# A recurrent-memory attention block with gMLP: the two halves' value sums side by side, their memory sums in other banks, 20 paired heads of Wo

## The chip, the core and the metric

The kernel runs on one core of a Trainium2 chip. The metric is device time in microseconds (us) of one launch; lower is better. Engines are named as in the profile: PE (TensorE, matmul), PEld (its weight loads), DVE (VectorE), ACT (ScalarE), POOL (GpSimd), SP (which issues DMAs).

## The reference

Two layers, each an attention block A and a gated MLP block B, each behind a layernorm and with a residual. Block A walks through 2048 rows in 64 segments of 32 rows, one after the other, since each takes 8 memory rows from the one before:

```python
for s in range(n_seg):                       # 64 segments, seg_len = 32
    xs = x[:, s * seg_len:(s + 1) * seg_len, :]
    h = jnp.concatenate([mem, xs], axis=1)   # 8 + 32 rows of 512
    q, k, v = h @ Wq, h @ Wk, h @ Wv         # 32 heads of 128
    scores = einsum(q, k) * scale            # masked: memory or not later
    o = softmax(scores) @ v
    o = einsum('bhte,hed->btd', o, Wo)
    mem = o[:, :M, :]                        # 8 rows, for the next segment
    outs.append(o[:, M:, :])
```

Block B is `z = gelu(x @ w_in)`, a spatial product of its normalised second half with `w_sp`, a gate and `w_out`.

## The kernel before

The work of PE, DVE and ACT stands in program order, written out by hand (`manual_schedule`); POOL and SP are ordered by the framework, which also puts in the waits. A PSUM tile of a pool with one buffer takes the banks of the tile before it under the same tag, and its first writer waits until the last reader of that one is done.

A segment (`segment`, called 64 times in each A block) does in order on PE:

1. psQ, psm and psK, later psV: q, k and v of the two halves r of 16 heads each, six products of 16 matmuls (L697), each 128 rows by 32 columns of the array, four side by side. ACT copies each to SBUF (L906), DVE transposes it into QQ or KA (L909).
2. psS, the scores of half 0 (L932, L936), psV (L697, the values of half 1), the scores of half 1. ACT takes Exp of each half (L941), DVE multiplies it with the mask into E (L944). psV goes through a DVE cast to VA.
3. A filler, then for half 0: `sums_memory` (L958, a matmul with ones that sums the softmax's denominators of the memory rows), `pv` (L975, L978, E times V into psO[0]), `memory_out` (ACT Ln and Exp of the sums, L992 and L993, and DVE's multiplication into uT, L994). These matmuls use 64 rows by 128 columns of the array.
4. A second filler, then the same for half 1 and `sums_tokens` (L967, the other denominators, into psT).
5. `wo_pairs` (L777, px): 18 heads of Wo, two heads of two halves side by side, 256 columns; `wo_rest` (L784): the other 14 heads, 128 columns each, into a free corner of psO[0].
6. A third filler. Beside it ACT copies half of px (cross, L1053), takes Ln of psT (Rt, L1055) and Exp of that (L1058); DVE folds px (L873, L875), adds psO's corner (`build_hA`, L880) and transposes the sum into hT (L881). These are the memory rows, and psQ of the next segment needs them.
7. DVE multiplies the token rows (`tok_out` L997, `last_out` L1000) out of psO with Rt.

PSUM: tag att (two banks) holds psQ, psS and psT in turn; attO0 holds psK and psO[0], attO1 psO[1]; accB holds psm, psV, px; accA the fillers' psb.

The fillers are pieces of a generator that `fill` advances. In the first three segments of each 128 rows it is `b_units`, which prepares q, k and v of rows that the next four segments use (six products j, two in a segment); in the fourth it is `y_part` (a piece of Wo's product for the finished rows, tile pwB) or, in four segments of each A block, nothing. `b_units` yields after 4, after 8 more and after 20 more matmuls of a pair of products; the copy out of PSUM (L751 or L758) is put on the list `copies`, which `run(copies)` empties in front of `wo_pairs` and after the third filler.

`spare1`, `spare2` and `spare3` put statistics, sums and layernorms of other rows between these steps, on DVE and POOL.

Of the kernel before, what the change touches and what calls it, by code (L numbers as in the profile page):

```python
# [8 lines left out]
F32 = mybir.dt.float32  # L9
ACT = mybir.ActivationFunctionType  # L10
ALU = mybir.AluOpType
# [3 lines left out]
P = 128  # L15
# [10 lines left out]
LN_EXP_SET = 6  # L26
GELU_SET = 11
WO_LOW = (4, 4, 4, 3)
WO_PAIR = 18
OLD_SIZES = (H * P, 8 * DH, H * 32, H * 32)  # L30
ORDERED = {mybir.EngineType.PE, mybir.EngineType.DVE, mybir.EngineType.Activation}

# [620 lines left out]
def a_block(tc, c, rows, front, MV_in, RS_in, MV_out, RS_out, ahead, wo, S, first):  # L653
    nc = tc.nc
# [5 lines left out]
    with ExitStack() as ctx:  # L660
# [75 lines left out]
        def b_units(tb, early=0):  # L736
            bs = blk_state[tb]
            order = (0, 2, 1, 3, 4, 5) if early else (4, 5, 0, 2, 1, 3)

            for k, j in enumerate(order):  # L740
                now = k < early
                ps = (accB if k % 2 and not (now and j == 5) else accA).tile([P, 512], F32, name="psb")[:]
                for kts in (((0,), (1, 2), (3,)), ((0, 1, 2, 3),))[k % 2]:
                    mm_chunk(ps, lambda kt, cg: bs["hB"][:, kt, :],
                             lambda kt, cg: qk_rhs(w, j, kt, cg) if j < 4 and now else cols_rhs(w, j, kt, cg), kts)
                    if kts[-1] != KT - 1:
                        yield

                def out(k=k, j=j, ps=ps, now=now):
                    if j >= 4:  # L750
                        nc.scalar.copy(bs["VB"][:, :, j - 4, :], ps.rearrange("p (i e) -> p i e", i=4))  # L751
                        if now:
                            ahead.regroup(bs["VB"], bs["VX"], (j - 4,))
                        elif j == 4:
                            store_v(bs)
                        return
                    r = rowsB[:, k % 2, :]
                    nc.scalar.copy(r, ps)  # L758
                    t = bs[("QTB", "KTB")[j // 2]][:, j % 2]
                    if now:  # L760
                        turns.append(lambda: nc.vector.transpose(out=t.rearrange("p a b -> p (a b)"), in_=r))
                    else:
                        nc.sync.dma_start_transpose(out=t.rearrange("p (i g) k -> p i (g k)", g=4), in_=r.rearrange("t (i e) -> t i e", i=4))

                if now or k % 2 == 0:
                    copies.append(out)
                else:
                    copies.insert(0, out)
                if now or k % 2:
                    yield  # L770

        def wo_pairs(px, lhs):

# [26 lines left out]
        def y_part(G, q, last=False):  # L800

            groups = [oBs[G][:, :, 32 * g:32 * g + 32] for g in range(4)]
            if last:
                parts = [[(groups[g], 8 * q + k) for g in range(3)] + [(groups[q], 24 + k)] for k in range(8)]
            else:
                parts = [[(groups[g], 8 * q + k) for g in range(4)] for k in range(8)]
            pwB = accA.tile([P, DM], F32, name="pwB")
            for k, _ in enumerate(wo_last(parts, pwB)):
                if k in (0, 2):
                    yield  # L810

            def add(lo, n, src):
                nc.vector.tensor_tensor(out=yB[G][lo:lo + n, :], in0=pwB[src:src + n, :], in1=yB[G][lo:lo + n, :], op=ALU.add)

            def out():
                n = 96 if last else P
                if q == 0:
                    yB[G] = wk.tile([P, DM], F32, name="yB", bufs=1)
                    nc.vector.tensor_copy(yB[G][0:n, :], pwB[0:n, :])
                else:  # L820
                    add(0, n, 0)
                if last:
                    if q == 2:
                        store_last(G, 0, 64, nc.sync)
                    add(32 * q, 32, 96)
                    if q == 2:
                        store_last(G, 64, 96, nc.sync)
                elif q == 3 and G < NB // 4 - 2:
                    stores.append(lambda: store_last(G, 0, P, nc.sync))
                elif q == 3:  # L830
                    store_last(G, 0, P, nc.sync)

            adds.append(out)
            yield
# [42 lines left out]
        def build_hA(s, pw, t1):  # L877

            t, at = memT[s % 2], 32 * (s % 4)
            nc.vector.tensor_tensor(out=t[:], in0=pw, in1=t1[:], op=ALU.add)  # L880
            nc.vector.transpose(out=rows.hT[s // 4][:, :, at:at + 32], in_=t[:])  # L881

        def store_o(s, pw, t1):

# [4 lines left out]
        def segment(s, fill, spare1, spare2, spare3, tail, loads):  # L889
# [56 lines left out]
            def e_all(e, lo, hi):  # L946

                return e[:, :, 0:160].rearrange("p n (i q) -> p n i q", q=40)[:, :, :, lo:hi]

            def e_own(e, b):  # L950
                return e[:, :, 160:224].rearrange("p n (i b e) -> p n i b e", i=4, b=2)[:, :, :, b, :]

            def sums_memory(r):

                for k in range(2):
                    for g in range(2):
                        e = E[64 * g:64 * g + 64, r]
                        nc.tensor.matmul(psO[r][:, g, 320:384], lhsT=ones[64 * g:64 * g + 64, :], rhs=e_own(e, 0) if k else e_all(e, 0, 8),  # L958
                                         start=(k == 0), stop=True, skip_group_check=True)

            def sums_tokens(ps):

                for k in range(2):
                    for g in range(2):
                        e = E[64 * g:64 * g + 64].rearrange("p r s n -> p (r s) n")
                        o = ps[:, g, :].rearrange("p (n i q) -> p n i q", n=4, i=4)
                        nc.tensor.matmul(o[:, :, :, 24:32] if k else o, lhsT=ones[64 * g:64 * g + 64, :],  # L967
                                         rhs=e_own(e, 1) if k else e_all(e, 8, 40), start=(k == 0), stop=True, skip_group_check=True)

            def pv(r):  # L970

                for i in range(4):
                    for g in range(2):
                        o = psO[r][:, g, 0:320].rearrange("p (s i q) -> p s i q", s=2, i=4)[:, :, i, :]
                        nc.tensor.matmul(o, lhsT=VA[64 * g:64 * g + 64, r, i, :], rhs=E[64 * g:64 * g + 64, r, :, 40 * i:40 * i + 40],  # L975
                                         start=False, stop=True, skip_group_check=True)
                for g in range(2):
                    nc.tensor.matmul(ends(heads40(psO[r][:, g, 0:320])), lhsT=VX[64 * g:64 * g + 64, j4, r, :],  # L978
                                     rhs=E[64 * g:64 * g + 64, r, :, 160:224], start=False, stop=True, skip_group_check=True)
# [7 lines left out]
            def rview(r, lo, hi):  # L987
                return Rt[:].rearrange("p g (r n q) -> p r g n q", r=2, q=32)[:, r, :, :, lo:hi]

            def memory_out(r):  # L990
                rm = Rm[:, r]
                nc.scalar.activation(out=rm, in_=psO[r][:, :, 320:384], func=ACT.Ln)  # L992
                nc.scalar.activation(out=rm, in_=rm, func=ACT.Exp, scale=-1.0)  # L993
                nc.vector.tensor_tensor(out=hview(uT_cur[:], r, 24, 32), in0=oview(r, 0, 8), in1=rm.rearrange("p g (n q) -> p g n q", q=8), op=ALU.mult)  # L994

# [35 lines left out]

            psO = [attO[r].tile([P, 2, 512], F32, name="psO") for r in range(2)]
            Rm = segp.tile([P, 2, 2, 64], F32, name="Rm", bufs=1)
            if not (first and s == 0):
                fill()
            sums_memory(0)
            pv(0)
            memory_out(0)
            spare1(E)
            if not (first and s == 0):  # L1040
                fill()
            sums_memory(1)
            pv(1)
            psT = att.tile([P, 2, 512], F32, name="psT")
            sums_tokens(psT)
            memory_out(1)
            run(copies)
            px = accB.tile([P, 512], F32, name="px")
            wo_pairs(px, uT_cur)
# [31 lines left out]
        if first:  # L1081
            for tb in range(2):
                ln_turn(tb, nc.scalar.copy)
            units, units1 = b_units(0, 6), b_units(1, 2)
            for gen in (units, units1, units):
                for _ in range(4):
                    next(gen)
                    run(turns)
                    run(copies)
                run(turns)  # L1090
        else:
            blk_state[0] = dict(KTB=KTBr[0], QTB=QTBr[0], VB=VBr[0], VX=wo.VX[0])
# [7 lines left out]
            rows.y_load(y, first, nc.gpsimd, rows.pool.tile([P, DM], F32, name="y_x")[:], o)()  # L1100

        def values(units):
            for n in (3, 1):
                for _ in range(n):
                    next(units)
                run(copies)
                yield
# [151 lines left out]
```

## Time and profile before

| | us |
|---|---|
| runs | 1649.05, 1649.40, 1654.26; median 1649.4 |
| profiled execution | 1649.51, span 1647.8 from first to last instruction |
| PE busy | 1590.4 (97%) |
| DVE, ACT busy | 1183.4 (72%), 1072.7 (65%) |
| granted TensorE clock | 0.997 of full speed |
| one regular segment, first psQ to first psQ | 10.16 (310.00 to 320.16) |
| PE, DVE, ACT busy in it | 10.16, 7.18, 8.18 |
| first block B, pz to the next psQ | from 706.80 to 848.50 |

128 segments of about 10.2 us make up most of the time, so 0.04 us in each is about 5 us in all. In the timeline a row gives start, duration, engine, line, what is written and read, the part of the array (128\*32 is 128 rows by 32 columns), the shape and how many such instructions follow each other; behind it, in brackets, the engine's idle time and what ended it. A duration of several matmuls reaches from the first start to the last modelled end, so rows overlap, and it is the starts that tell PE's pace.

### The profile page before, as it was taken

How to read it: one execution, taken by the hardware profiler on the slowest of the kernel's cores; microseconds unless marked ns; L12 is line 12 of the kernel's file. 1: busy time of each engine (PE TensorE's matmuls, PEld its weight loads, DVE VectorE, ACT ScalarE, POOL GpSimd, SP SyncE). 2: the span in 40 equal slices, each digit the busy share in tenths (PEclk: the TensorE clock that was granted, in tenths of full speed). 3: DMA queues.
4: the chain of work that ended last, by engine and by line, in shares of the span. 5: the costliest groups of instructions: out<-in, count | busy, mean ns of one | idle time of the engine just before them, and what ended most of it. 6: DMA issues, size and time to landing. Idle time of an engine off the chain costs nothing.

```text
span 1647.8 us, 87178 instructions
## 1 busy us (share of the span) xinstructions
PE 1590.4 (97%) x39122; PEld 953.7 (58%) x39122; DVE 1183.4 (72%) x2924; ACT 1072.7 (65%) x2278; POOL 289.2 (18%) x604
## 2 busy tenths in 40 slices
PE   4799999999999999999999999999999999999999
PEld 1455555555665666566655565556556666554565
DVE  3677777778887787884467777777788778877722
ACT  2577777777777777661047777777777777776400
POOL 5111111111211122320011111111122112214000
PEclk9999999999999999999999999999999999999999
DMA  9312221212222234276952121112233123335796
GB/s 353 101 42 42 43 42 44 44 42 74 78 55 45 73 84 87 87 190 139 211 168 46 46 45 46 49 46 44 60 88 85 46 58 94 97 63 153 150 198 162
DMA packets 264734, 149.06 MB, mean 90 GB/s; under 512 B 198680, under 2 KB 240784, under 8 KB 264360
## 3 DMA queue, kind: packets, MB, share of 16 engines
q1 hardware_dynamic: 251128, 99.66, 27.6%
q0 software_dynamic: 13232, 43.82, 8.2%
q8 instruction: 307, 5.03, 1.3%
q14 instruction: 67, 0.55, 0.1%
HBM read 59.68 MB, written 37.19 MB: 59 GB/s over the span
## 4 chain that ended last, share of the span: by engine, by line
PE 55%; DVE 2%; issue 0%; ACT 0%; DVEq 0%
PE pg L388 9%; PE psQ L697 7%; PE psK L697 7%; PE psb L697 5%; PE pz L287 5%; PE px L777 4%; PE psm L697 3%; PE psV L697 3%; PE psO L784 3%; PE py L431 2%; PE pwB L796 2%; PE psO L958 1%; PE psO L975 1%; PE psT L967 1%; PE psS L932 1%; PE pw L1211 0%
## 5 line engine op out<-in xcount | busy, mean ns | idle before, releaser
L697 PEld LDWEIGHTS <-hT 128*32 128x32 bf16 x12288 | 339.8, 97 | 299.9 <-DVE hT L881 27.8
L909 DVE STREAM_TRANSPOSE QQ<-rows 128x512 bf16<-128x512 bf16 x256 | 177.6, 694 | 60.0 <-ACT rows L906 59.0
L909 DVE STREAM_TRANSPOSE KA<-rows 128x512 bf16<-128x512 bf16 x256 | 176.0, 688 | 11.6 <-ACT rows L906 6.1
L997 DVE TENSOR_TENSOR uT<-psO,Rt 128x384 bf16<-128x384 f32 x256 | 141.0, 551 | 36.6 <-ACT Rt L1058 35.6
L906 ACT CAST rows<-psQ 128x512 bf16<-128x512 f32 x256 | 142.8, 595 | 28.3 <-PE psQ L697 25.2
L388 PE MATMUL pg<-z,wspT 128*128 128x344 bf16 x1024 | 154.3, 309 | 0.0
L1058 ACT ACTIVATE Rt<-Rt 128x512 f32<-128x512 f32 x256 | 147.2, 622 | 4.0
L697 PE MATMUL psQ<-Wq_sb,hT 128*32 128x512 bf16 x2048 | 136.0, 383 | 10.7 <-DVE hT L881 6.7
L941 ACT ACTIVATE S<-psS 128x224 bf16<-128x224 f32 x256 | 91.5, 358 | 80.6 <-PE psS L936 80.5
L994 DVE TENSOR_TENSOR uT<-psO,Rm 128x128 bf16<-128x128 f32 x256 | 74.7, 292 | 96.6 <-ACT Rm L993 95.9
L867 POOL COPY KX<-old 128x128 bf16<-128x128 bf16 x128 | 70.2, 548 | 392.3 <-PE psS L936 272.7
L777 PEld LDWEIGHTS <-uT 128*32 128x32 bf16 x4608 | 110.5, 96 | 47.5 <-DVE uT L994 31.7
L697 PE MATMUL psQ<-Wk_sb,hT 128*32 128x512 bf16 x2048 | 135.7, 382 | 0.0
L777 PE MATMUL px<-Wo,uT 128*32 128x256 bf16 x3840 | 134.7, 274 | 0.2 <-DMA Wo<-in_A_Wo_dram 0.2
L697 PE MATMUL psm<-Wq_sb,hT 128*32 128x512 bf16 x2048 | 134.4, 379 | 0.0
L697 PE MATMUL psK<-Wk_sb,hT 128*32 128x512 bf16 x2048 | 134.4, 379 | 0.0
L697 PE MATMUL psK<-Wv_sb,hT 128*32 128x512 bf16 x2048 | 134.3, 379 | 0.0
L697 PE MATMUL psV<-Wv_sb,hT 128*32 128x512 bf16 x2048 | 133.6, 378 | 0.0
L784 PE MATMUL psO<-Wo_high,uT 128*32 128x128 bf16 x7168 | 126.7, 220 | 7.0 <-issue 4.4
L1055 ACT ACTIVATE Rt<-psT 128x1024 f32<-128x1024 f32 x128 | 131.2, 1025 | 3.2
L867 POOL COPY KX<-front 128x128 bf16<-128x128 bf16 x126 | 67.5, 542 | 373.2 <-PE psS L936 238.0
L388 PEld LDWEIGHTS <-wspT 128*128 128x128 bf16 x1024 | 100.2, 98 | 53.2
(190 smaller groups left out, 2867.2 us busy)
## 6 DMA issues: line engine op xcount, KB each, us to landing
o_d<-o_sb SPq DMA_DIRECT2D x126, 64.0 KB
vb_d<-front SPq DMA_DIRECT2D x30, 256.0 KB
VX<-vb_d SPq DMA_DIRECT2D x120, 64.0 KB
ln_x<-xd SPq DMA_DIRECT2D x26, 256.0 KB
y_o<-o_d POOLq DMA_DIRECT2D x22, 256.0 KB, 3.3
xd<-y_o POOLq DMA_DIRECT2D x22, 256.0 KB, 2.9
Wq_sb<-in_A_Wq_dram POOLq DMA_DIRECT2D x8, 512.0 KB, 9.3
Wk_sb<-in_A_Wk_dram POOLq DMA_DIRECT2D x8, 512.0 KB, 11.0
```

Of the source, the lines that this page charges most:

```text
L287: nc.tensor.matmul(pz[:, c0:c1], lhsT=xnT[:, kt, :], rhs=w_in_sb[:, kt, c0:c1], start=(kt == 0), stop=(kt == KT - 1))
L388: nc.tensor.matmul(pg[t][:, k, 0:344], lhsT=wsp[t][:, st, :], rhs=z(st, 344 * k, 344 * k + 344), start=(st == 0), stop=(st == NT - 1))
L697: return [nc.tensor.matmul(ps[32 * cg:32 * cg + 32, :], lhsT=lhs(kt, cg), rhs=rhs(kt, cg), start=(kt == 0), stop=(kt == KT - 1), tile_posi ...
L777: nc.tensor.matmul(px[at:at + 32, 0:256], lhsT=lhs[:, h, :], rhs=wo_rhs(h, slice(k + 2, None, -2) if h % 2 else slice(k, None, 2)), start= ...
L784: nc.tensor.matmul(pw[32 * cg:32 * cg + 32, :], lhsT=lhs[:, h, :], rhs=wo_rhs(h, cg), start=False, stop=(h == H - 1), tile_position=(0, 32 ...
L867: eng.tensor_copy(KX[:, :, r].rearrange("p g (k i) -> p i g k", i=4), bs["KTB"][:, r].rearrange("p (i g) k -> p i g k", i=4)[:, :, :, 8 * ...
L906: return r, mms, nc.scalar.copy(r[:], ps)
L909: nc.vector.transpose(out=QQ[:, j % 2, :, 0:32] if j < 2 else KA[:, j % 2], in_=r[:])
L941: return nc.scalar.activation(out=S[:, r], in_=psS[:, r, 0:224], func=ACT.Exp, scale=scale)
L997: nc.vector.tensor_tensor(out=hview(uT_nxt[:], r, 0, 24), in0=oview(r, 8, 32), in1=rview(r, 0, 24), op=ALU.mult)
L1055: nc.scalar.activation(out=Rt[:], in_=psT[:], func=ACT.Ln)
L1058: nc.scalar.activation(out=rt, in_=rt, func=ACT.Exp, scale=-1.0)
```

## The change

- `pv(1)` follows `pv(0)` at once (`spare1`, between them in the text, holds no PE work), then `sums_memory(1)`, `sums_tokens` and `memory_out(1)`; the second filler comes after them, in front of `wo_pairs`.
- `sums_memory(0)` goes into the first 64 columns of psT, which `sums_tokens` overwrites later; `sums_memory(1)` stays in psO[1] but after `pv(1)`. So `pv` clears its bank itself (`start=(i == 0)`).
- The fillers are cut 12, 4 and 16 matmuls instead of 4, 8 and 20, for `b_units` and for `y_part`. Outside the first rows both products of a pair use accA, and each is copied out after its own filler: the first now in front of `wo_pairs`. The store of V follows product 5 instead of 4.
- 20 heads of Wo go in pairs, 12 singly.
- `build_hA` adds and transposes in two halves of 64 columns.

```diff
-WO_PAIR = 18
+WO_PAIR = 20
...
-                ps = (accB if k % 2 and not (now and j == 5) else accA).tile([P, 512], F32, name="psb")[:]
-                for kts in (((0,), (1, 2), (3,)), ((0, 1, 2, 3),))[k % 2]:
+                ps = (accB if now and k % 2 and j != 5 else accA).tile([P, 512], F32, name="psb")[:]
+                for kts in (((0, 1, 2), (3,)), ((0, 1, 2, 3),))[k % 2]:
...
-                        elif j == 4:
+                        elif j == 5:
                             store_v(bs)
...
-                if now or k % 2 == 0:
-                    copies.append(out)
-                else:
-                    copies.insert(0, out)
-                if now or k % 2:
-                    yield
+                copies.insert(len(copies) if now else 0, out)
+                yield
...
             for k, _ in enumerate(wo_last(parts, pwB)):
-                if k in (0, 2):
+                if k in (2, 3):
                     yield
...
-            nc.vector.tensor_tensor(out=t[:], in0=pw, in1=t1[:], op=ALU.add)
-            nc.vector.transpose(out=rows.hT[s // 4][:, :, at:at + 32], in_=t[:])
+            for k in range(2):
+                half = slice(64 * k, 64 * k + 64)
+                nc.vector.tensor_tensor(out=t[:, half], in0=pw[:, half], in1=t1[:, half], op=ALU.add)
+                nc.vector.transpose(out=rows.hT[s // 4][:, 2 * k:2 * k + 2, at:at + 32], in_=t[:, half])
...
-            def sums_memory(r):
+            def sums_memory(r, ps, fresh):
...
-                        nc.tensor.matmul(psO[r][:, g, 320:384], lhsT=ones[64 * g:64 * g + 64, :], rhs=e_own(e, 0) if k else e_all(e, 0, 8),
-                                         start=(k == 0), stop=True, skip_group_check=True)
+                        nc.tensor.matmul(ps[:, g, :], lhsT=ones[64 * g:64 * g + 64, :], rhs=e_own(e, 0) if k else e_all(e, 0, 8),
+                                         start=(fresh and k == 0), stop=True, skip_group_check=True)
...
                         nc.tensor.matmul(o, lhsT=VA[64 * g:64 * g + 64, r, i, :], rhs=E[64 * g:64 * g + 64, r, :, 40 * i:40 * i + 40],
-                                         start=False, stop=True, skip_group_check=True)
+                                         start=(i == 0), stop=True, skip_group_check=True)
...
-                nc.scalar.activation(out=rm, in_=psO[r][:, :, 320:384], func=ACT.Ln)
+                nc.scalar.activation(out=rm, in_=ps, func=ACT.Ln)
...
+            psT = att.tile([P, 2, 512], F32, name="psT")
+            sums = (psT[:, :, 0:64], psO[1][:, :, 320:384])
             if not (first and s == 0):
                 fill()
-            sums_memory(0)
+            sums_memory(0, sums[0], True)
             pv(0)
-            memory_out(0)
+            memory_out(0, sums[0])
             spare1(E)
+            pv(1)
+            sums_memory(1, sums[1], False)
+            sums_tokens(psT)
+            memory_out(1, sums[1])
             if not (first and s == 0):
                 fill()
-            sums_memory(1)
-            pv(1)
-            psT = att.tile([P, 2, 512], F32, name="psT")
-            sums_tokens(psT)
-            memory_out(1)
             run(copies)
```

At the start of the first block the number of steps taken from the generators goes from 4 to 3 (and 3 to 2), since a pair of products now has three yields; the matmuls there stay the same.

More of the change, by code (lines that the diff above doesn't have):

```diff
@@ L988, in rview, with memory_out @@
                 return Rt[:].rearrange("p g (r n q) -> p r g n q", r=2, q=32)[:, r, :, :, lo:hi]
-            def memory_out(r):
+            def memory_out(r, ps):
                 rm = Rm[:, r]
-                nc.scalar.activation(out=rm, in_=psO[r][:, :, 320:384], func=ACT.Ln)
+                nc.scalar.activation(out=rm, in_=ps, func=ACT.Ln)
                 nc.scalar.activation(out=rm, in_=rm, func=ACT.Exp, scale=-1.0)
@@ L1085, in a_block @@
             for gen in (units, units1, units):
-                for _ in range(4):
+                for _ in range(3):
                     next(gen)
@@ L1102, in values @@
         def values(units):
-            for n in (3, 1):
+            for n in (2, 1):
                 for _ in range(n):
```

## The prediction

> **What bounds the kernel now.** I read the page first: TensorE (PE) is busy nearly throughout, and the chain that ended last is PE work.
>
> ```profile
> PE   1590.4 (97%) x39122; PEld 953.7 (58%) x39122; DVE 1183.4 (72%) x2924; ACT 1072.7 (65%) x2278; POOL 289.2 (18%) x604
> PE 55%; DVE 2%; issue 0%; ACT 0%; DVEq 0%
> ```
>
> A busy PE need not be a PE that streams columns, so I read one regular segment in the timeline of each engine. From one first psQ to the next (310.00 to 320.16) it takes 10.16 us; the median over both A blocks is 10.17. PE around the change:
>
> ```profile
> 315.44 0.39 PE L697 MATMUL psb<-Wq_sb,hB 128*32 128x512 bf16 x4
> 315.76 0.23 PE L958 MATMUL psO<-E,ones 64*128 64x64 bf16 x4
> 315.83 0.31 PE L975 MATMUL psO<-E,VA 64*128 64x80 bf16 x8
> 315.97 0.22 PE L978 MATMUL psO<-E,VX 64*128 64x128 bf16 x2
> 316.12 0.62 PE L697 MATMUL psb<-Wq_sb,hB 128*32 128x512 bf16 x8
> 316.67 0.23 PE L958 MATMUL psO<-E,ones 64*128 64x64 bf16 x4
> 316.94 0.43 PE L967 MATMUL psT<-E,ones 64*128 64x512 bf16 x4
> 317.31 1.05 PE L777 MATMUL px<-Wo,uT 128*32 128x256 bf16 x30
> ```
>
> Four 512-column matmuls run side by side and take 0.216 us (16 of them, psQ to psQ, 0.864). Yet the filler of four takes 0.32 until L958, and the filler of eight 0.55 instead of 0.43. VX, 0.05 us of columns, takes 0.15 when a filler follows (315.97 to 316.12) and 0.06 when psT follows. So each change between 128\*32 and 64\*128 costs PE about **0.095 us**, and a segment with two fillers has four of them.
>
> Beside it run ACT and DVE:
>
> ```profile
> 315.73 0.36 ACT L941 ACTIVATE S<-psS 128x224 bf16<-128x224 f32 x1 [0.16 <-PE psS L936]
> 316.24 0.28 ACT L992 ACTIVATE Rm<-psO 128x128 f32<-128x128 f32 x1
> 318.52 0.26 ACT L1053 COPY cross<-px 64x128 f32<-64x128 f32 x1 [0.76 <-PE px L777]
> 318.81 1.03 ACT L1055 ACTIVATE Rt<-psT 128x1024 f32<-128x1024 f32 x1
> ```
>
> ```profile
> 316.14 0.38 DVE L944 TENSOR_TENSOR E<-S,maskN 128x448 bf16<-128x448 bf16 x1
> 316.89 0.29 DVE L994 TENSOR_TENSOR uT<-psO,Rm 128x128 bf16<-128x128 f32 x1 [0.37 <-ACT Rm L993]
> 319.31 0.29 DVE L880 TENSOR_TENSOR memT<-psO,t 128x128 bf16<-128x128 f32 x1
> 319.64 0.31 DVE L881 STREAM_TRANSPOSE hT<-memT 128x128 bf16<-128x128 bf16 x1
> ```
>
> The reader is to see when each releases PE: E's second half is done at 316.52 and PE uses it at 316.67; Rt's first Ln has read psT by 319.84, and psQ, which takes psT's banks, begins at 320.16. Both have slack today. The change spends it.
>
> **Part 1: fewer changes of shape.** pv(0), pv(1), sums_memory(1) and sums_tokens stand in one run, so two of the four changes go: −0.19 us a segment. If that were all, 117 regular segments with fillers would give −22 us.
>
> **Part 2: what ends last before px.** The first filler is now 12 matmuls, so sums_memory(0) is due at 315.44 + 0.65 + 0.10 = 316.19. It writes psT, which needs the banks of psS: L941 ends at 316.09, and ACT to PE takes 0.05 (at the start a copy of hB ends at 17.57 and psb begins at 17.62), so 316.14, hidden by 0.05. By the spacing above pv(1) could follow at 316.19 + 0.265 = 316.46. It needs E's second half: 316.52 plus 0.05 (in a segment without fillers E ends at 123.03 and L958 begins at 123.08) = **316.58**, a new wait of 0.12. From there the same matmuls as between 316.67 and 317.31, in another order, take 0.633: filler of four at 317.21, px possible at 317.43.
>
> px also needs the first half of uT. From the start of Ln (L992, 316.24) to the end of the multiplication (L994, 317.18) it takes 0.944. Today Ln waits for VX, in the same tile, and begins 0.042 after VX's end (median over all segments). Now it waits for the sums in psT alone: last one at 316.24, 0.19 long, then 0.042, so 316.47, 0.23 later than now, because the filler before grew by 0.43. Then uT at 317.41, px at **317.47**. That 0.042 is the uncertain price: after the short matmuls of psS the Exp begins 0.114 after their end (315.42 + 0.20 to 315.73), so I keep 0.042 to 0.114 as bounds, 317.47 to 317.54, and take 0.06 because the four other such waits of ACT and DVE here lie at 0.04 to 0.055. The Trainium skill ("TensorE: Matmul & The Clock Gate", Part 3, The cost: per-tile semaphore tail) fits the time from a matmul's end to its signal as a constant, a part per tile and 26 ns per increment; with two tiles and one increment an estimate of 0.061. By that rule alone the sum below would be +2 us, by the row of VX 0 us; the trace has VX at 0.042, below the rule, and Exp above it.
>
> Result: px begins 0.16 to 0.24 later than at 317.31, with 16 filler matmuls done by then instead of 12, which is 0.216 of work.
>
> **Part 3: from px to the next psQ,** now 2.854 us. PE: px goes from 9 to 10 groups of 256 columns (0.99/9 = 0.110 each), 1.10; the other heads from 56 to 48 matmuls at 0.78/56, 0.67; the last filler from 20 to 16, 0.864; together **2.64**. Moving two heads costs nothing in itself (0.110 against 0.112). But px ends 0.11 later, and on ACT the copy of cross and Rt's Ln stand behind it: 1.21 + 0.11 = 1.33, + 0.29 to Rt, + 1.03, + 0.05 to PE = **2.69**. psT's banks are then free 0.05 after PE would want them. The third chain is hA: the last of psO at 1.726, its end and signal 0.27, so 2.00; t1 ends at 1.90 + 0.11 and lets the add begin at 2.04. Halves are not in the trace: 64 columns less are 0.07 less (128x384 against 128x128 at L997 and L1000: 551 and 280 ns for 256 columns), so 0.22 and 0.25. First half of hT at 2.55, with signal 2.60, hidden; second at 3.03, needed after psQ's first eight matmuls at 2.69 + 0.43 = 3.12, hidden by 0.09. Bounds: no saving by halving (0.29 and 0.31 each) puts the second at 3.29 and psQ's third row of weights 0.17 late.
>
> So psQ follows px by 2.69 instead of 2.85: −0.16. Against +0.16 to +0.24 that is **0.00 to +0.08 us a segment**.
>
> **Part 4: what moves beside it.** The copy of psb after the second filler (0.575, L758 or L751) stands on ACT behind the second Exp of Rm (ends about 317.74) and is done by 318.35, ahead of cross at 318.80: hidden; without that cover Rt would slip by its length. The last filler shares its bank and begins at 319.24: hidden. The store of V and the transposing DMAs of rowsB that follow that copy are issued on SP up to 2 us earlier, before the store of o_sb, and are wanted segments later: nothing. The bank that psm, psV and px share gets no filler any more: no new wait. DVE gets two more instructions, 0.3 us, and Rt's chain moves by 0.27 against psQ, so the last outputs end 2.07 after psQ instead of 1.79; the first row to be transposed comes at 2.09 to 2.34: hidden in regular segments, and where DVE has a sum for yB besides (2.38 now), the last transposition still ends 0.2 before the second scores. The eight segments without fillers lose 0.1 to 0.2 each, since px waits for uT there: +1 us.
>
> Where PE waited for instructions after px (29 segments, 8.5 us in all, L784 "issue") the 0.05 of Rt is covered: −1.6 us, in the sum below.
>
> **Sum.** Applied to every segment's own offsets in this trace: 0.0 us at 0.042, +2.1 at 0.06, +8.3 at 0.114. The profiled execution took 1649.51 (span 1647.8 plus 1.7 around it), the median of the runs is 1649.4. Forecast 1649.5 + 2.1 = **1651.5 us**. A measurement of this kernel can tell about 0.3% (5 us) from no change.
>
> **Rivals.**
> - *The saving comes through.* If neither uT nor Rt binds, px is at 317.43 and psQ 2.64 later: −0.094 × 117 = −11, 1638.5. For: PE now shows no waits for either, and the 0.042 may be less where no long run follows. Against: 0.94 and 1.03 are fixed durations, and Rt's Ln must end before psQ. 0.15.
> - *uT is late* (slower): at 0.114 after the short sums PE stands at px for 0.11 us in each segment, 1657.7. It decides from about 0.09 on. For: the row of psS has just such short matmuls. Against: VX. 0.27.
> - *psQ waits for both halves of hT* (slower), if the scheduler doesn't tell the halves apart: 3.03 instead of 2.69, +39, 1689. Against: px begins today while the second half of uT is still being written (317.31, L994 again at 317.80). Or the halves save nothing: +0.17 × 117, 1670. Together 0.11.
> - *The balance*, within 0.3%: 0.47.
>
> The likeliest by itself is 1645 to 1655. For eight in ten I take 1640 to 1664, which leaves out both cases of the halves and the lower end of the first rival. Faster by over 0.3%: 0.15; within: 0.47; slower: 0.38.
>
> **What would show it.** Right: regular segments near 10.16 to 10.20; the two gaps beside the middle filler gone; PE idle 0.12 before the second L975 behind E; px about 0.16 later in the segment, its weight load released by L994; psQ released by ACT L1055. Wrong: regular segments at 10.07 or less (no chain binds), a longer delay from the short sums to L992, or psQ released by the second transposition into hT.

## The result, and the profile after

| | before | after |
|---|---|---|
| runs on one chip, us | 1649.4 median (1648.57 to 1654.56, 9 runs) | 1645.34 median (1643.32 to 1646.87, 9 runs) |
| profiled execution, us | 1649.51 (span 1647.8) | 1643.32 (span 1641.6) |
| regular segment, median, us | 10.17 | 10.165 |

The ratio is 0.9967, with a 95% interval of 0.9955 to 0.9979: the changed kernel is faster by 0.33%, where 1651.5 had been forecast. Yet the regular segment, at 10.165 us, stands where the forecast put it (10.16 to 10.20). So the gain lies where the median segment doesn't show it. One run of the experiment e13 below, of 5187 us, is left out of its median.

The page of after, where PE is still what ends last:

```profile
PE 1585.8 (97%) x38610; PEld 953.5 (58%) x38610; DVE 1207.2 (74%) x3176; ACT 1074.9 (65%) x2278; POOL 290.0 (18%) x604
PE 55%; DVE 2%; ACT 1%; issue 0%; DMA 0%; DVEq 0%
```

The timeline of PE in one regular segment of after, the stretch that was shown of before:

```profile
313.95 0.83 PE L697 MATMUL psb<-Wq_sb,hB 128*32 128x512 bf16 x12
314.71 0.23 PE L956 MATMUL psT<-E,ones 64*128 64x64 bf16 x4
314.78 0.31 PE L973 MATMUL psO<-E,VA 64*128 64x80 bf16 x8
314.92 0.22 PE L976 MATMUL psO<-E,VX 64*128 64x128 bf16 x2
315.09 0.32 PE L973 MATMUL psO<-E,VA 64*128 64x80 bf16 x8
...
315.35 0.45 PE L965 MATMUL psT<-E,ones 64*128 64x512 bf16 x4
315.73 0.40 PE L697 MATMUL psb<-Wq_sb,hB 128*32 128x512 bf16 x4
315.98 1.05 PE L773 MATMUL px<-Wo,uT 128*32 128x256 bf16 x30
...
318.67 0.59 PE L697 MATMUL psQ<-Wq_sb,hT 128*32 128x512 bf16 x5
```

Between the fillers all value sums now stand in one run. The only hole in it is ahead of the second L973: VX to L973 takes 0.17 us. Before, VX of the second half began at 316.88 and L967 at 316.94, 0.06 later:

```profile
316.88 0.22 PE L978 MATMUL psO<-E,VX 64*128 64x128 bf16 x2
```

DVE in the same segment:

```profile
314.66 0.38 DVE L942 TENSOR_TENSOR E<-S,maskN 128x448 bf16<-128x448 bf16 x1
315.64 0.29 DVE L992 TENSOR_TENSOR uT<-psO,Rm 128x128 bf16<-128x128 f32 x1 [0.60 <-ACT Rm L991]
...
318.09 0.23 DVE L878 TENSOR_TENSOR memT<-psO,t 128x64 bf16<-128x64 f32 x1
318.35 0.24 DVE L879 STREAM_TRANSPOSE hT<-memT 128x64 bf16<-128x64 bf16 x1
318.52 0.18 DVE L878 TENSOR_TENSOR memT<-psO,t 128x64 bf16<-128x64 f32 x1
318.74 0.24 DVE L879 STREAM_TRANSPOSE hT<-memT 128x64 bf16<-128x64 bf16 x1
```

E's second half ends at 315.04 and L973 follows 0.05 later; uT's first half ends at 315.93 and px follows 0.05 later. At the segment's end Rt's Ln, in the timeline of ACT, runs from 317.60 to 318.62, and psQ begins 0.05 behind it:

```profile
317.60 1.02 ACT L1054 ACTIVATE Rt<-psT 128x1024 f32<-128x1024 f32 x1
```

Meanwhile the first half of hT is ready at 318.59, and the second at 318.98.

Where the time went shows in the rows of one line, the 128-column matmuls of `wo_rest` (L784 before, L780 after). Before, the matmuls, and what ended the idle time ahead of them and of their weight loads (PE and PEld are added up, so a hole can count twice):

```profile
L784 PE MATMUL psO<-Wo_high,uT x7168: 216/219/314, 48.9 to 1505.5; 128*32 128x128 bf16 x200
...
  issue: 14.1, 26
```

and after:

```profile
L780 PE MATMUL psO<-Wo_high,uT x6144: 219/219/314, 48.8 to 1499.2; 128*32 128x128 bf16 x199
...
  issue: 3.1, 3
```

"issue" is time in which the engine waited for nothing that the profile shows; the figures are us and times. In the first segment waits of 2 to 3 us stand in every kernel; that segment is left out of what follows. Taken from the starts of neighbouring matmuls (a hole of over 0.08 us counts, here and below), PE stood still **within** this run for 8.1 us in 18 places before, and 0.7 us in 2 places after. One of the 18, in the timeline of PE:

```profile
369.16 0.68 PE L784 MATMUL psO<-Wo_high,uT 128*32 128x128 bf16 x36
370.44 0.46 PE L784 MATMUL psO<-Wo_high,uT 128*32 128x128 bf16 x20 [0.60 <-issue]
```

and the DMA queues between 368.07 and 369.06, the last time ahead of it that queue 8 moved anything:

```profile
q8 instruction: 1, 0.02, 6.0%
```

That queue brings PE's instructions, in pieces of 16 KB: 307 pieces, 5.03 MB in before (302 pieces in after), for 78591 matmuls, weight loads and semaphore instructions, so a piece holds 256 of them. All 18 holes stand at the same place of this stream, counted in 256s, to within one: at the border of two pieces. And PE goes on 1.2 to 1.6 us after the piece has landed: here it landed at 369.05, and 370.44 − 369.05 = 1.39.

Segment by segment, the 17 regular segments that had a hole before became 6.0 us shorter in all (the 18th hole is in the last segment), the 100 others with fillers 1.3 us (the median one was 0.003 longer), and the eight without fillers 0.8 us longer. So the gain is in the segments that had the holes. The holes vary between executions: in a second profile (e14 and e15 below) the unchanged kernel before had 4.9 us of them, the kernel after 0.2.

### The profile page after: what moved, and what is told of

The parts are those of the page before. It is cut to its first block, busy times and chain, and to the rows that moved or that the text cites. A ratio compares the mean times of both kernels' runs of the same rounds, so it can differ in the third digit from the quotient of the medians.

```text
span 1641.6 us, 86352 instructions
## 1 busy us (share of the span) xinstructions
PE 1585.8 (97%) x38610; PEld 953.5 (58%) x38610; DVE 1207.2 (74%) x3176; ACT 1074.9 (65%) x2278; POOL 290.0 (18%) x604
## 4 chain that ended last, share of the span: by engine, by line
PE 55%; DVE 2%; ACT 1%; issue 0%; DMA 0%; DVEq 0%
PE pg L388 9%; PE psQ L697 7%; PE psK L697 7%; PE psb L697 5%; PE px L773 4%; PE pz L287 4%; PE psV L697 3%; PE psm L697 3%; PE psO L780 2%; PE py L431 2%; PE psO L973 2%; PE pwB L792 1%; PE psT L965 1%; PE psS L930 1%; PE psT L956 1%; PE pw L1210 0%
## 5 line engine op out<-in xcount | busy, mean ns | idle before, releaser
L697 PEld LDWEIGHTS <-hT 128*32 128x32 bf16 x12288 | 328.6, 96 | 318.6 <-DVE hT L879 84.2
L773 PEld LDWEIGHTS <-uT 128*32 128x32 bf16 x5120 | 125.3, 96 | 26.9 <-DVE uT L992 13.3
L1054 ACT ACTIVATE Rt<-psT 128x1024 f32<-128x1024 f32 x128 | 131.1, 1024 | 3.2
L697 PEld LDWEIGHTS <-hB 128*32 128x32 bf16 x2976 | 70.1, 96 | 81.3 <-issue 30.4
```

What stands on the lines that cost most here:

```text
L697: return [nc.tensor.matmul(ps[32 * cg:32 * cg + 32, :], lhsT=lhs(kt, cg), rhs=rhs(kt, cg), start=(kt == 0), stop=(kt == KT - 1), tile_posi ...
L773: nc.tensor.matmul(px[at:at + 32, 0:256], lhsT=lhs[:, h, :], rhs=wo_rhs(h, slice(k + 2, None, -2) if h % 2 else slice(k, None, 2)), start= ...
L1054: nc.scalar.activation(out=Rt[:], in_=psT[:], func=ACT.Ln)
```

## The experiments

All ratios are to the kernel before on the same chip, with 95% intervals. Lines are those of each kernel. Two theories of why the holes went stand at the start. A: after has fewer of the dense 128-column matmuls (48 instead of 56) in which the supply of instructions falls behind. B: PE's new waits, for E and for uT, give the supply time. C came up on the way: it is the new order itself, by the place in the stream at which each piece is asked for.

**e1_after_wo18.** The kernel after, 18 pairs.

```diff
-WO_PAIR = 20
+WO_PAIR = 18
```

> The changed kernel with 18 heads in pairs again, all else as changed. Both theories have the regular segment shorter, since px ends 0.11 us earlier and Rt's Ln frees psT's banks before PE wants them: psQ 2.64 after px instead of 2.69, a segment of 10.11 instead of 10.16, -6 us. Theory A (PE ran short of instructions in the run of 128-column matmuls of Wo, and 48 instead of 56 of them cured it): the gaps inside that run come back from 0.6 us to about 7 us in all, so 1645 to 1647. Theory B (the new waits of PE at E, uT and psQ gave the supply of instructions time to run ahead): the gaps stay near 1 us, so about 1639.

1637.45, ratio 0.9916 (0.9903 to 0.9929): faster than both kernels. Segments take 10.10. The row of `wo_rest` says

```profile
L780 PE MATMUL psO<-Wo_high,uT x7168: 219/219/314, 49.1 to 1494.7; 128*32 128x128 bf16 x200
...
  issue: 2.1, 1
```

All 56 matmuls are back and the holes are not (0.1 us in one place): A falls. And the px to psQ stretch, in the timeline:

```profile
314.99 1.05 PE L773 MATMUL px<-Wo,uT 128*32 128x256 bf16 x30
...
317.63 1.03 PE L697 MATMUL psQ<-Wq_sb,hT 128*32 128x512 bf16 x16
```

2.64 instead of 2.69: with px shorter by 0.11, Rt comes early enough and PE's own work sets the pace.

**e2_before_wo20.** The kernel before with `WO_PAIR = 20`.

> The kernel before with 20 heads in pairs and nothing else. Its regular segment stays at 10.16 by both (psQ 2.85 after px, Rt's chain at 2.69 is hidden). Theory A: the gaps inside the run of 128-column matmuls fall from 7.3 us to below 2, so about 1643.5. Theory B: they stay, 1649.

1654.98, ratio 1.0024 (1.0010 to 1.0037); segments 10.24; holes 4.1 us in 10 places. Both theories missed it: px to psQ grew to 2.92. The third filler's second product shares its bank with px in the kernel before, and waits until DVE has folded px (L875 ends 321.40):

```profile
321.11 0.29 DVE L875 TENSOR_TENSOR t<-px,cross 128x128 f32<-128x128 f32 x1
```

```profile
321.16 0.39 PE L697 MATMUL psb<-Wq_sb,hB 128*32 128x512 bf16 x4
321.45 1.05 PE L697 MATMUL psb<-Wk_sb,hB 128*32 128x512 bf16 x16
```

The four matmuls of 321.16 should take 0.22 and took 0.29. The new use of the banks, with no filler beside px, spares the 20 pairs this wait.

**e3_before_wo14.** The kernel before with `WO_PAIR = 14`: more single heads, so 72 dense matmuls instead of 56.

> The kernel before with 14 heads in pairs, 72 single 128-column matmuls in a run instead of 56. PE work as before within 0.01 us a segment. Theory A: the gaps grow, by 5 to 15 us in all, so 1655 to 1665. Theory B: unchanged, 1649.

1653.22, ratio 1.0019 (1.0009 to 1.0028); segments 10.19; holes 13.4 us in 26 places. The holes do grow with the length of the dense run, in the old order, and the time lies between the theories' figures.

**e4_order_only.** The change without its last two parts: 18 pairs, and `build_hA` whole.

```diff
-WO_PAIR = 20
+WO_PAIR = 18
...
-            for k in range(2):
-                half = slice(64 * k, 64 * k + 64)
-                nc.vector.tensor_tensor(out=t[:, half], in0=pw[:, half], in1=t1[:, half], op=ALU.add)
-                nc.vector.transpose(out=rows.hT[s // 4][:, 2 * k:2 * k + 2, at:at + 32], in_=t[:, half])
+            nc.vector.tensor_tensor(out=t[:], in0=pw, in1=t1[:], op=ALU.add)
+            nc.vector.transpose(out=rows.hT[s // 4][:, :, at:at + 32], in_=t[:])
```

> The order of the value sums, the sums' banks and the cut of the fillers as changed, but 18 heads in pairs and hA added and transposed whole. Regular segment: px at 2.04 after the scores as in the changed kernel; hT whole is ready at 2.00 + 0.64 + 0.05 = 2.69 after px, so 10.16 again. Theory A: gaps as before the change, 7 us, so 1649. Theory B: gaps near 1 us, 1644 to 1646.

1647.63, ratio 0.9976 (0.9967 to 0.9984); segments 10.17, holes 0.6 us in 2 places. Order, banks and filler cut alone take the holes away, against A.

**e5_before_late_E** and **e6_before_late_E_wo14.** The kernel before with one more DVE instruction ahead of the second multiplication into E, with 18 and with 14 pairs: PE has to wait for E, in the old order.

```diff
+        idle = pers.tile([P, 200], F32, name="idle")
...
+            nc.vector.memset(idle[:], 0.0)
```

> The kernel before with one DVE memset of 200 elements in front of the second mask product, so that E's second half comes about 0.24 us later (1.34 instead of 1.10 after the last matmul of the scores). PE's instructions are the same, one for one; PE now stands about 0.14 us in front of sums_memory(1), as the changed kernel does in front of pv(1), and px moves from 1.88 to 2.02. Regular segment 10.30, +16 us. Theory B (a wait of PE in front of px lets the supply of instructions run ahead): the gaps inside the run of 128-column matmuls of Wo fall from 7.3 us to below 2, so about 1660. Theory C (the gaps hang on the order of PE's instructions, which this kernel leaves alone): they stay at 7, so 1666.

> The same memset in the kernel before with 14 heads in pairs, where the gaps were 12.3 us in 26 places. Theory B: below 4 us, so about 1661. Theory C: 12 us, so about 1669.

1655.95, ratio 1.0029 (1.0017 to 1.0041), holes 5.5 us in 14 places; and 1661.55, ratio 1.0068 (1.0049 to 1.0087), 11.1 us in 23. The memset took 0.23 us and made PE wait 0.07, less than was meant, so these leave B open.

**e9_before_later_E.** The same with the memset twice.

> The kernel before with that memset (225 ns) twice, so PE stands about 0.28 us in front of sums_memory(1) instead of 0.07 with one and nothing without. Regular segment 10.44, +33 us. Theory B: the gaps in Wo's run go on falling, 7.3 us with no wait, 4.9 with 0.07, below 1.5 with 0.28, as in the changed kernel, whose waits come to 0.19 a segment: about 1677. Theory C: near 5, about 1681.

1693.95, ratio 1.0270 (1.0252 to 1.0289). Now PE waits for E in every segment:

```profile
PE psO L959 <- DVE E L945: 51.7, 127, 2.7
```

0.4 us each; segments take 10.56, and the holes are down to 1.2 us in 6 places. A long enough wait does give the supply its time, as B has it. (The time lies above the figure expected because the wait is 0.40 and not 0.28.) It is a bad bargain: 51.7 us of waiting for some 5 us of holes.

**e7_wo18_reciprocal** and **e8_reciprocal_split_E.** e1 with a DVE reciprocal in place of ACT's Ln and Exp of the memory sums, to bring uT, and with it px, forward; in e8 the second multiplication into E is split as well.

```diff
-                nc.scalar.activation(out=rm, in_=ps, func=ACT.Ln)
-                nc.scalar.activation(out=rm, in_=rm, func=ACT.Exp, scale=-1.0)
+                nc.vector.reciprocal(out=rm, in_=ps)
```

> The changed kernel with 18 paired heads, and the memory sums inverted by one DVE reciprocal out of PSUM instead of Ln and Exp on ACT. uT's first half is ready at about 1.75 after the scores instead of 1.99, so px no longer waits for it: it begins at 2.00 (E's wait of 0.12 in front of pv(1) stays) instead of 2.04, psQ 2.64 later. Regular segment 10.06 to 10.07, 4 to 5 us less than with Ln and Exp, about 1633. By theory B the gaps in Wo's run stay below 2 us, since the wait for E stays.

> As the kernel with the reciprocal, and E's second half written in two DVE instructions, columns 0 to 160 first: pv(1) can begin at about 1.05 instead of 1.15, where PE is ready at 1.03. px at 1.90 and a regular segment of 9.96, 12 us less than with the reciprocal alone, if nothing else binds. Now PE stands nearly nowhere, as in the kernel before. Theory B: the gaps inside Wo's run come back, 4 us or more, so about 1626. Theory C: below 2, so about 1621.

1753.48, ratio 1.0625 (1.0611 to 1.0639), and 1765.98, ratio 1.0703 (1.0687 to 1.0719): clear misses. DVE's groups in e7:

```profile
L990 DVE RECIPROCAL Rm<-psT 128x128 f32<-128x128 f32 x128 | 122.4, 956 | 0.0
```

0.96 us for what takes 0.59 on ACT, and on the engine that also makes uT: px came at 2.66 us after the last scores instead of 2.04. Neither has a hole, but with a wait that long they can't tell the theories apart.

**e11_wo18_split_E.** e1 with the second half of E in two pieces of 160 and 64 columns.

```diff
-                nc.vector.tensor_tensor(out=E[:, r], in0=S[:, r].unsqueeze(1).to_broadcast([P, 2, 224]), in1=maskN[:], op=ALU.mult)
+                for lo, hi in ((0, 224),) if r == 0 else ((0, 160), (160, 224)):
+                    nc.vector.tensor_tensor(out=E[:, r, :, lo:hi], in0=S[:, r, lo:hi].unsqueeze(1).to_broadcast([P, 2, hi - lo]),
+                                            in1=maskN[:, :, lo:hi], op=ALU.mult)
```

> The changed kernel with 18 paired heads and only E's second half in two instructions. pv(1) begins at about 1.09 instead of 1.15, but px still waits for uT at 2.04, so the regular segment stays at 10.10 and the time at 1637. If it is E that holds px, px moves to 1.98 and the time to 1630.

1636.01, ratio 0.9914 (0.9893 to 0.9934), the same as e1. The second pv begins 1.09 after the last scores instead of 1.15, and px at 2.04 as before: uT, not E, holds px.

**e10_split_E_no_ln.** e11 without the Ln, so that uT is computed from wrong factors, 0.3 us earlier.

> The changed kernel with 18 paired heads, with E's second half written in two DVE instructions, and with the Ln of the memory sums left out (Exp alone, so the memory rows are not the reference's). uT's first half is ready at about 1.65 and pv(1) can begin at about 1.09, so px begins at 1.94 instead of 2.04 and psQ 2.64 later: a regular segment of 10.00. PE's instructions are those of the kernel with 18 pairs, which had 0.1 us of gaps in Wo's run; their order is the changed one, but the waits are nearly gone (0.05 instead of 0.16). Theory B: gaps come back, 3 us or more, about 1629. Theory C: below 1, about 1626.

1629.41, ratio 0.9880 (0.9862 to 0.9897); segments 10.08, holes 0.2 us in one place. Meant as the order without PE's waits, it still waited for E's second piece, and px came at 2.03 instead of the 1.94 expected.

**e12_after_whole_hA.** The kernel after with 20 pairs and `build_hA` whole.

> The changed kernel, 20 pairs, with hA added and transposed whole as before. t1 ends 2.01 after px and the add begins 0.10 later; whole, hT is ready at 2.11 + 0.33 + 0.31 + 0.05 = 2.80, after Rt (2.69): psQ 0.11 later in each segment, +13 us against the changed kernel, about 1658. If the halves save nothing it stays at 1645.

1658.66, ratio 1.0054 (1.0037 to 1.0071); segments 10.28 and px to psQ 2.805. In the timelines of DVE and PE psQ (321.96) now stands behind the whole transposition, 0.06 after its end, with Rt's Ln done at 321.79:

```profile
321.59 0.31 DVE L877 STREAM_TRANSPOSE hT<-memT 128x128 bf16<-128x128 bf16 x1
```

```profile
321.96 1.05 PE L697 MATMUL psQ<-Wq_sb,hT 128*32 128x512 bf16 x16
```

With after, e1 and e4 this makes a table of the new order (time, and px to psQ, us):

| | 18 pairs | 20 pairs |
|---|---|---|
| `build_hA` whole | 1647.63, 2.696 | 1658.66, 2.805 |
| in halves | 1637.45, 2.638 | 1645.34, 2.690 |

The four were measured on several chips, so their differences are best taken from the ratios: the halves are worth 10 us with 18 pairs and 14 with 20, and the two more pairs cost 8 us with halves and 13 without.

**e13_no_waits.** e1 without the waits: the second half's sums read the first half's E (so half 1 is computed from half 0's weights) and the Ln is left out, as in e10.

> The changed kernel with 18 paired heads, in which the second half's value and memory sums read the first half's E and the Ln of the memory sums is left out (so neither values nor memory rows are the reference's). PE's instructions and their order are those of the changed kernel with 18 pairs; pv(1) needs no new E and begins at 1.03, px at 1.88, psQ 2.64 later: no wait in a regular segment, which takes 9.94. Theory B: gaps in Wo's run come back, 4 us or more, about 1623. Theory C: below 1 us, about 1619.

1623.40, ratio 0.9842 (0.9827 to 0.9857); segments 10.03. The second pv stands 0.06 behind VX, so PE doesn't wait for E:

```profile
311.98 0.22 PE L976 MATMUL psO<-E,VX 64*128 64x128 bf16 x2
312.04 0.31 PE L973 MATMUL psO<-E,VA 64*128 64x80 bf16 x8
```

One wait of 0.07 was left, ahead of `sums_tokens`. The holes are 0.7 us in one place. The time is B's figure, but the holes, which are what the theories differ by, are C's. A wait of 0.07 in the old order (e5) left 5.5 us of them, so in the new order they stay away without the help of the waits.

**e14_before_again** and **e15_after_again.** Both kernels unchanged, to see how much the holes vary.

> The kernel before once more, unchanged. If the gaps in Wo's run belong to the kernel, they are 5 to 9 us again, in 14 to 22 places; if they are chance of one execution, anything from 0 to 12.

> The changed kernel once more, unchanged: gaps below 1.5 us if they belong to the kernel. Time 0.996 to 0.998 of the kernel before, as measured first.

Before: 1647.79 in one run, 4.9 us in 11 places ("issue: 9.0, 18" in the row of `wo_rest`, against 14.1, 26 at first), just below the range expected. After: 1644.46, ratio 0.9970 (0.9957 to 0.9982), 0.2 us in 2 places.

**e16_old_order_new_cut** and **e17_new_order_old_cut.** One half of the new order each, with 18 pairs and `build_hA` whole. e16: before, with the diff's edits of the fillers alone. e17: e4 with those edits undone, so that the value sums stand side by side but the fillers are cut 4, 8 and 20 as before. The edit is that part of the change (undone in e17; what the expectations call 12, 4 and 16 heads are matmuls):

```diff
-                for kts in (((0,), (1, 2), (3,)), ((0, 1, 2, 3),))[k % 2]:
+                for kts in (((0, 1, 2), (3,)), ((0, 1, 2, 3),))[k % 2]:
...
-                if k in (0, 2):
+                if k in (2, 3):
```

> The kernel before with its own order of the two value sums and its own banks' order, 18 pairs and whole hA, but with the fillers cut 12, 4 and 16 heads and all three in accA. In that order px now stands behind a shorter last filler, and waits for uT at about T + 2.24 instead of 1.88, so that a regular segment should take about 10.3 to 10.4 us by both theories. They differ in PE's waits for instructions within Wo's run of 128-column matmuls. Theory F (the length of the first filler decides when the next 16 KB of instructions are asked for): under 1.5 us of gaps in Wo's runs over the whole kernel. Theory O (the order of the value sums decides): 4 to 8 us, as in the kernel before.

> The kernel after's order of the value sums (side by side, no filler between them), 18 pairs and whole hA, but with the fillers cut 4, 8 and 20 heads as before. sums_memory(0) stands again right behind the first exps, so px should come at about T + 2.22 and a regular segment take about 10.4 to 10.5 us by both theories. Theory F (the length of the first filler): the gaps in Wo's runs come back, 4 to 8 us. Theory O (the order of the value sums): under 1.5 us.

1669.35, ratio 1.0121 (1.0092 to 1.0150), segments 10.37, holes 1.1 us in 5 places; and 1684.32, ratio 1.0212 (1.0182 to 1.0241), segments 10.50, 0.1 us in one. Both segments come out as worked out, but not by one cause. In e16 px waits 0.14 us for uT. In e17 uT is ready 0.31 ahead of px, and it is `sums_memory(0)` that waits in every segment, until the second Exp has read psS, whose banks psT takes:

```profile
PE psT L958 <- ACT S L941: 41.0, 128, 0.5
```

The holes stay away in both, so by them alone neither F nor O is left out; by e9 a wait ahead of px can drive them away. How late the pieces come tells more. The table is for the pieces whose border falls in the last 41 instructions (some 20 matmuls) of `wo_rest`, 17 to 21 in each profile, and gives medians in us: how long PE takes from the border before to this one, with the holes taken out, and when in this time the transfer of the next piece begins.

| kernel | PE's time | transfer begins | holes in all |
|---|---|---|---|
| before, e14 | 3.48, 3.40 | 1.35, 1.22 | 8.1, 4.9 |
| e5 | 3.54 | 1.10 | 5.5 |
| e9 | 3.85 | 1.21 | 1.2 |
| e16 | 3.73 | 1.17 | 1.1 |
| after, e15 | 3.62, 3.64 | 0.69, 0.80 | 0.7, 0.2 |
| e1, e4 | 3.60, 3.60 | 0.75, 0.79 | 0.1, 0.6 |
| e13 | 3.53 | 0.78 | 0.7 |
| e17 | 3.82 | 0.74 | 0.1 |

A transfer that begins at 1.35, takes 1.1 and is followed by the 1.2 that PE needs at the least after the landing lets PE go on at 3.65, later than its 3.48: a hole. One that begins at 0.75 lets it go on at 3.05, and there is none. e9 and e16 get by with the late transfer since PE takes longer (theory B). e13 has nearly the time of before and gets by with the early transfer (theory C). All kernels in the old order lie at 1.10 to 1.35 (e2, e3 and e6 at 1.11 to 1.15), all in the new one at 0.69 to 0.80. So the instructions come some 0.4 us earlier with the new order of the value sums, whatever the cut of the fillers. The sums' other banks go with that order in every run and are not told apart from it.

What sets the start of a transfer wasn't settled. One lead stands in the traces, untested: each kernel in the old order has a semaphore instruction in every segment of PE's stream in front of `sums_memory(0)`, and no kernel in the new order has one there. In before:

```profile
L958 PEldq EVENT_SEMAPHORE  x128: 51/51/51, 40.8 to 1500.6; - x128
```

Of the transfers of before 35 begin 1.0 to 1.5 us after this instruction, where later half microseconds hold 14 on average; in the other profiles of the old order it is 29 to 37. No run has the old order without this wait, so the order itself and the wait that comes with it remain two rivals.

## Why the prediction was wrong

The predicted time and sign were wrong (1651.5; measured 1645.34, inside the stated 1640 to 1664), by a term that the working had treated as small. Point by point:

- **Two of the four changes of shape go.** Right: the holes beside the middle filler are gone.
- **pv(1) waits for E.** Right: it follows the last scores by 1.152 (forecast 1.153), sums_memory(0) by 0.769 (0.769).
- **px waits for uT.** Right in mechanism; the delay from the sums to Ln was **0.043** and not the 0.06 chosen. Ln comes at 1.044 (1.046 at 0.042), px at 2.040 after the last scores (2.043). The rival at 0.114 falls, and with it the row of psS as a model. The rule of the Trainium skill ("TensorE: Matmul & The Clock Gate", Part 3, The cost: per-tile semaphore tail) would give an estimate of 0.061; the trace has 0.043, so the row of VX (0.042) was the one to go by. The choice was worth 2.1 us, and with it the sign of the forecast, since the sum was 0.0 at 0.042; the four waits of 0.04 to 0.055 that the prediction gave as its reason don't reach 0.06 either.
- **px to psQ by Rt.** Right: 2.690 (2.694), behind L1054; e1 shows that PE alone would take 2.638 (2.64).
- **Halves of hT.** Right: add 0.225 in the first half and 0.185 in the second (0.22), transposition 0.245 (0.25). The first half is done 2.62 behind px (2.55), the second 3.01, or 3.06 with 0.05 for the signal (3.03), needed at 3.12. Without the halves, by the ratio of e12, 14 us would be lost.
- **Segments without fillers.** Right: the eight take 10.10; five stood at 9.91 and three at 10.11 to 10.15 before, so +0.8 us in all (forecast +1).
- **"Where PE waited for instructions after px (29 segments, 8.5 us in all, L784 "issue") the 0.05 of Rt is covered: −1.6 us."** This step failed. It took the holes as given and counted only how much of each the new slack would cover. They nearly all went: −7.4 us in the first pair of profiles (8.1 to 0.7), −4.7 in the second (4.9 to 0.2).

With the sum's own parts: 0.0 us at the delay that held, of which −1.6 was this step. Put −7.4 in its place: 0.0 + 1.6 − 7.4 = −5.8 us; the profiled execution became 6.2 shorter. For the second pair: 0.0 + 1.6 − 4.7 = −3.1, and those profiled executions differ by 2.4 (1647.79 and 1645.41); the medians of nine runs differ by 4.1. So the term accounts for the result in size. That it is the new order that drives the holes out, and not the fewer matmuls or PE's waits, is shown by e1, e4 and e13, and the earlier transfers show how. Why they begin earlier, and which part of the new order does it, stays open.

The rival "the saving comes through" named the right sign, but for a reason that the runs deny: uT and Rt both bind.

The change also hides a loss: two more pairs lengthen px by 0.11, and Rt's Ln, which must read psT before psQ may have its banks, stands behind px. The prediction had both figures, 2.64 for PE and 2.69 for Rt, and didn't draw the conclusion that 18 pairs would be better by 0.05 in each segment. e1 has it: −8 us.

## What to carry to other kernels

When a dense engine has idle time put down to "issue", treat it as a term that the change may remove (8.1 to 0.7 us here) or enlarge (13.4 in e3). Give it both ends, nothing and all of it, and look where in the stream it stands. A median segment hides it, so compare the sum of the segments with the median too. Where three chains meet at one point (here PE 2.64, Rt 2.69, the first half of hT with its signal 2.67 after px), an edit that shortens one and lengthens another by the same amount is a loss. The new wait of ACT behind short matmuls was priced best here by the row with the same part of the array (VX, 0.042), not by the other short matmuls (0.114); that is one case.

## What the runs showed of the hardware

- PE's instructions came in 16 KB pieces of 256 instructions, each some 1.1 us on its queue (median of before); in none of the ten profiles that hold all matmuls did PE go on into a piece sooner than 1.2 us after it had landed. In a run of 56 matmuls of 14 ns each (0.78 us) that left holes of up to 1.4 us, 4.9 and 8.1 us in two executions of the same program.
- A DVE reciprocal of 128x128 f32 took 0.94 to 0.96 us, three times the multiplication of the same size (0.29).
- Half the columns don't halve a DVE instruction: 128x64 took 0.225 or 0.185 us to add and 0.245 to transpose, against 0.29 and 0.31 for 128x128.
